# Turns of one operation for a background conversion, and the second head's preparation behind the second maximum, in a fused attention and expert kernel

## The chip, the cores and the metric

The kernel runs on one core of a Trainium2 chip. The metric is the time of one execution on the device in microseconds (us). Before the change the median of three runs is 1062.84 us (1062.28 to 1064.66). Engines are named as the profile names them: PE (TensorE, matrix products and transposes), DVE (VectorE), ACT (ScalarE), POOL (GpSimd), and SP, the queue that issues nearly all transfers.

## The reference

Three stages, each fed by the one before:

```python
q_pool = q.reshape(B, H, S // 2, 2, D).mean(axis=3)        # 4 x 8 heads, 576 pooled queries, D = 64
scores = np.matmul(q_pool, k.transpose(0, 1, 3, 2)) / sqrt(D)   # 576 x 1152
attn = softmax(scores);  x = attn @ v                      # 2304 rows of 512
# experts: 8, one per row by argmax of x @ w_gate, only rows with x @ w_skip > 0
x[rows] += gate * (relu(x[rows] @ w1[e]) @ w2[e])
# dense: out = ((x @ m1) * (x @ m2) @ w3) @ w_out          # weights arrive as 64-bit floats
```

## The kernel before

Attention fills the first half of the time. The 32 heads are taken in 16 pairs p of two heads, each pair in nine *tiles* l: eight of 128 queries of one head, and one (l = 4) with the last 64 queries of both. There are 144 tiles i = 9p + l, and the main loop takes two in a *step* (a = 0, 2, 4, ...). Products are made in fp32r from a high and a low part (a rounded copy, and what is left), so queries and keys are first split in two.

For one tile: PE multiplies queries by the keys (`emit_s`, L271) into three banks of PSUM, DVE finds the negated maximum of a row over all 1152 scores (`emit_x`, L282), ACT takes the exponential (`emit_e`, L294), PE transposes the result in nine pieces (`emit_t`, L305) into the three banks that the tile two further on will use for its scores, and ACT, DVE, ACT copy those three banks away (`emit_c`, L324: the second bank is DVE's). PE multiplies the copies by the values (`emit_pv`, L341).

Every engine works through its own instructions in the order in which the loop writes them. In step a this is: the exponentials of tiles a-2 and a-1; a turn of side work (the *first place*); the value products of earlier tiles; the 18 transposes of tiles a-2 and a-1 with their copies; a turn of side work again (the *second place*); the scores and maxima of tiles a and a+1. So DVE's order in a step is: first place, two copies, second place, two maxima.

Side work is of two kinds. The *routing* of a finished batch (`route_ops`) chooses experts, in pieces marked P (uses a PSUM bank), D (small DVE operations) and C. The *conversion* (`conv_ops`) turns the dense stage's 64-bit weights into 32-bit ones, in 40 chunks of 128 x 512 values: POOL squares the upper word (L96), and four DVE operations on data in SBUF make the result, L111 and L112 (mask and shift of the exponent), L116 (sign) and L119 (lower bits); SP stores it. A generator hands these out: an even chunk takes two turns (L111 with L112, L116 with L119), an odd chunk three (L111 with L112, L116, L119). Each place takes one turn, or a D piece of the routing in its stead.

At the start the first pair is prepared apart. `prep_q(h, DVE, 0, 256, ...)` and `prep_k(h, ...)` split the first 256 queries and the keys of head h on DVE (L203 to L207 and L197; ACT makes the keys' rounded copy, L196); POOL splits the other queries (same lines, POOL). For head 0 this stands ahead of the loop; for head 1, which tile 2 uses first, behind the scores and maximum of tile 0. `prep(1, 0)`, `prep(1, 1)` and `prep(1, 2)`, the split of the second pair's keys and queries, are POOL's (L224 to L238) and stand behind tiles 0, 1 and 2. Later pairs are split at tiles 6, 7 and 8 of the pair two before.

Of the kernel before, what the change touches and what calls it, by code (L numbers as in the profile page):

```python
# [17 lines left out]
NE, D, F = 8, 512, 1024  # L18
# [26 lines left out]
def body(ctx, tc, q, k, v, w9, w1, w2, m1, m2, w3t, wo, cst, mcst, ids, out, dbg=None):  # L45
# [3 lines left out]
    def f(t):  # L49
        return t.bitcast(F32)  # L50
# [37 lines left out]
    def conv_ops(erl):  # L88
        def ld(name, c):
            h = erl.tile([128, CW, 2], I32, tag="ch", name="ch", bufs=4)  # L90
            SP.dma_start(h, c_src(name, c))
            return h
        def sq(h):
            m = erl.tile([128, CW], F32, tag="cm", name="cm", bufs=3)
            hf = h.bitcast(F32)[:, :, 1]
            POOL.tensor_tensor(m, hf, hf, op=ALU.mult)  # L96
            return m

        nxt = [ld(*conv_q[i]) for i in range(3)]
        yield  # L100
        ms = [sq(nxt[0]), sq(nxt[1])]
        yield
        for n, (name, c) in enumerate(conv_q):
            h = nxt.pop(0)
            if n + 3 < len(conv_q):
                nxt.append(ld(*conv_q[n + 3]))
            a = erl.tile([128, CW], I32, tag="ca", name="ca", bufs=2)
            hf = h.bitcast(F32)[:, :, 1]
            m = ms.pop(0)
            u = m.bitcast(I32)  # L110
            DVE.scalar_tensor_tensor(m, m, TINY * TINY, hf, op0=ALU.is_ge, op1=ALU.mult)  # L111
            DVE.tensor_scalar(u, u, 0x07FFFFFF, 3, op0=ALU.bitwise_and, op1=ALU.logical_shift_left)  # L112
            yield
            if len(nxt) >= 2:
                ms.append(sq(nxt[1]))
            DVE.scalar_tensor_tensor(u, h[:, :, 1], -0x40000000, u, op0=ALU.bitwise_and, op1=ALU.bitwise_or)  # L116
            if n % 2:
                yield
            DVE.scalar_tensor_tensor(a, h[:, :, 0], 29, u, op0=ALU.logical_shift_right, op1=ALU.bitwise_or)  # L119
            c_dst(name, c, a.bitcast(F32))  # L120
            yield
# [13 lines left out]
    if True:  # L135
# [78 lines left out]
        def ld_kh(h):  # L214
            SP.dma_start(f(KH[0][64 * h:64 * h + 64]), f(KS[0][h][0:64]))

        def prep(p, j):
            if p >= NP:
                return
            i = p % 2  # L220
            if j == 0:
                for c in range(3):
                    cc = slice(384 * c, 384 * c + 384)
                    POOL.tensor_scalar(KH[i][:, cc], rawk[p][:, cc], 1.0, 0.0, op0=ALU.mult, op1=ALU.add)  # L224
                    POOL.tensor_tensor(KL[:, cc], rawk[p][:, cc], f(KH[i][:, cc]), op=ALU.subtract)  # L225
                del rawk[p]
            elif j == 1:
                qr = rawq.pop(p)
                s = pre[p] = erl.tile([128, SQ], F32, tag="qsum", name="qsum", bufs=1)
                POOL.tensor_tensor(s, qr[:, 0], qr[:, 1], op=ALU.add)  # L230
                POOL.tensor_scalar(s, s, 0.0625, 0.0, op0=ALU.mult, op1=ALU.add)
            elif j == 2:
                s = pre.pop(p)
                POOL.tensor_scalar(QN[0], s, 1.0, 0.0, op0=ALU.mult, op1=ALU.add)
                POOL.tensor_tensor(QN[1], s, f(QN[0]), op=ALU.subtract)
                for h in range(2):
                    r = slice(64 * h, 64 * h + 64)
                    POOL.tensor_scalar(BD[i][r, r], f(QN[1][r, 512:576]), 1.0, 0.0, op0=ALU.mult, op1=ALU.add)  # L238
            elif j == 3:
                for h in range(2):  # L240
                    r = slice(64 * h, 64 * h + 64)
                    for u, t in enumerate((KH[i], KL)):
                        SP.dma_start(f(KS[i][h][64 * u:64 * u + 64]), f(t[r]))
            else:
                for h in range(2):
                    r = slice(64 * h, 64 * h + 64)
                    for u in range(2):
                        d = slice(64 * u, 64 * u + 64)
                        if h == 0:
                            SP.dma_start(f(QS[i][h][0][d, 0:576]), f(QN[0][r]))  # L250
                        else:
                            SP.dma_start(f(QS[i][h][0][d, 0:512]), f(QN[0][r, 0:512]))
                            SP.dma_start(f(QS[i][h][0][d, 576:640]), f(QN[0][r, 512:576]))
                        SP.dma_start(f(QS[i][h][1][d]), f(QN[1][r]))
# [245 lines left out]
        conv = conv_ops(erl)  # L500
        rts = {}

        def side(kinds):
            k = rts.get("k")
            if k and k in kinds:
                rts["k"] = next(rts["g"], None)
            if kinds != "P" and k != "D":
                next(conv, None)

        def emit_meta(scratch):  # L510
# [240 lines left out]
        with tc.manual_schedule():  # L751
# [37 lines left out]
            for a in range(0, NSTEP + 8, 2):  # L789
                if a >= 44 and (a - 44) % 36 == 0 and (a - 44) // 36 < NB - 1:  # L790
                    rts["g"] = route_ops((a - 44) // 36)
                    rts["k"] = next(rts["g"])
                its = [i for i in (a - 2, a - 1) if 0 <= i < NSTEP]
                for i in its:
                    emit_e(i)
                route_step(a, 0)
                if a > 5:
                    side("DC")
                for pe in range(0, NP, 2):
                    for dp, hf, kt in PVU.get(a - 9 * pe, ()):  # L800
                        emit_pv(pe + dp, hf, kt)
                evac = {}
                for i in (a, a + 1):
                    if i < NSTEP or i - 2 in its:
                        st_s[i] = ps_s.tile([128, 3, 512], F32, tag="s", name="s")
                    evac[i] = []
                for i in its:
                    for g in range(3):
                        emit_t(i, g, i + 2, evac[i + 2])
                        emit_c(i, g, EV[g], evac[i + 2])  # L810
                if a > 5:
                    side("DC")
                route_step(a, 1)
                for i in (a, a + 1):
                    p, l = divmod(i, NT9)
                    ss = i < NSTEP
                    if i == NSTEP - NT9 + 1:
                        for _ in conv:
                            pass
                        ectx.close()  # L820
                        wfill = wprime_fill()
                    if i > NSTEP - NT9:
                        next(wfill, None)
                    if l == (4 if p == 0 else 1):
                        load(p + 2)
                    if l == 7 and p >= 1:
                        load_v(p + 1)
                    if ss:
                        for g in range(3):
                            emit_s(i, g, evac[i])  # L830
                        emit_x(i)
                        if i == 0:
                            prep_q(1, DVE, 0, 256, sq[1])
                            for c in range(3):
                                prep_k(1, 384 * c, 384 * c + 384)
                            ld_kh(1)
                            for h in range(2):
                                prep_q(h, POOL, 256, SQ, sr[h])
                            next(conv)
                            DVE.tensor_copy(base, cs[:, C_EOFF:C_EOFF + NC_])  # L840
                            DVE.tensor_copy(csr, cs[:, C_U:C_U + 256])
                        if i == 2:
                            PE.matmul(VB[1][:, 0:128], lhsT=ones, rhs=tri, start=True, stop=True)
                            DVE.tensor_copy(iota[:, 0:128], VB[1][:, 0:128])
                            DVE.tensor_scalar(iota[:, 128:NSL], iota[:, 0:NSL - 128], 128.0, None, op0=ALU.add)
                            DVE.tensor_scalar(idf, idt, 1.0, None, op0=ALU.add)
                    if ss and p == 0 and l < 3:
                        prep(1, l)
                    if i == 4:
                        next(conv)  # L850
                    if ss and l >= 6:
                        prep(p + 2, l - 6)
                    if ss and l in ((3, 4) if p == 0 else (4, 5)):
                        prep(p + 1, l if p == 0 else l - 1)
# [36 lines left out]
            n = 0  # L891
# [170 lines left out]
```

## Time and profile before

| what | value |
|---|---|
| median of three runs | 1062.84 us |
| the profiled execution | 1057.09 us |
| its span, first to last instruction | 1055.3 us |
| PE busy / DVE / ACT / POOL | 1003.0 / 600.0 / 460.7 / 386.7 us |
| mean granted TensorE clock | 0.988 of full |
| main loop (tiles) | until about 520 us of the span |

The profiled execution is one run of the program with the hardware profiler on, and lies 5.75 us under the median of the others. Busy time of PE counts matrix products that overlap; where PE waits, the row of its next instruction tells how long, and for whom.

### The profile page before, as it was taken

The numbers are of one execution on the slowest core, as the hardware profiler recorded it, in microseconds if no ns is written. First come the engines' busy times: TensorE is split into PE (matmuls) and PEld (weight loads), VectorE is DVE, ScalarE is ACT, GpSimd is POOL, SyncE is SP. The second block draws the span as 40 slices with busy tenths as digits, with TensorE's granted clock in tenths as the row PEclk, the third lists the DMA queues.
The fourth block names the chain that finished last, engine by engine and source line by source line (L and its number), as shares of the span: only waits on it lengthen the run. The fifth ranks groups of instructions, "written<-read, shape, count | busy, mean of one in ns | idle before, by whom it ended". The sixth has DMA issues, their size and how long they took to land. (4 is left out here: it accounts for less than half of the span.)

```text
span 1055.3 us, 16801 instructions
## 1 busy us (share of the span) xinstructions
PE 1003.0 (95%) x6101; PEld 834.5 (79%) x6101; DVE 600.0 (57%) x934; ACT 460.7 (44%) x902; POOL 386.7 (37%) x426
## 2 busy tenths in 40 slices
PE   4899999999999999999999999996999999999996
PEld 3677777777777777787778788874989898989895
DVE  5888988789889898866554424256523131313120
ACT  3566566655665566666522324254422121212120
POOL 4752444582536743460801625167111101010101
PEclk8999999999999999999989999998999999999999
DMA  9887878579964687743416723233101010110000
GB/s 263 225 237 210 241 214 216 164 191 246 253 197 149 193 253 210 191 117 116 159 40 224 279 62 135 97 138 129 31 20 41 25 37 31 31 37 24 30 1 32
DMA packets 68237, 144.82 MB, mean 137 GB/s; under 512 B 12960, under 2 KB 22560, under 8 KB 68130
## 3 DMA queue, kind: packets, MB, share of 16 engines
q1 hardware_dynamic: 63330, 129.28, 42.5%
q0 software_dynamic: 4800, 14.24, 4.1%
q8 instruction: 52, 0.85, 0.3%
q14 instruction: 55, 0.45, 0.1%
HBM read 86.21 MB, written 22.87 MB: 103 GB/s over the span
## 5 line engine op out<-in xcount | busy, mean ns | idle before, releaser
L294 ACT ACTIVATE p<-s,sm 128x1152 f32<-128x1152 f32 x144 | 175.9, 1221 | 183.3 <-DVE sm L282 183.3
L282 DVE TENSOR_REDUCE sm<-s 128x1 f32<-128x1152 f32 x144 | 189.1, 1349 | 20.2 <-PE s L271 17.6
L305 PEld LDWEIGHTS s<-cs,p 128*128 128x128 f32 x1296 | 140.3, 142 | 65.3 <-ACT p L294 57.7
L305 PE MATMUL s<-cs,p 128*128 128x128 f32 x1296 | 167.9, 279 | 21.7 <-ACT p L294 19.2
L271 PE MATMUL s<-k,q 128*128 128x384 f32 x864 | 178.6, 348 | 7.9 <-DVE k L197 7.7
L271 PEld LDWEIGHTS s<-k,q 128*128 128x128 f32 x864 | 149.9, 191 | 10.2 <-DVE k L197 8.2
L341 PE MATMUL vb<-pt,vr 128*64 128x256 f32 (+1 forms) x1152 | 155.1, 412 | 0.0
L972 DVE TENSOR_TENSOR ar<-b,ar 128x384 f32<-128x384 f32 x48 | 26.7, 557 | 192.2 <-PE b L968 192.2
L324 ACT COPY pt<-s 128x384 f32<-128x384 f32 x288 | 122.5, 491 | 11.3 <-PE s L305 9.2
L341 PEld LDWEIGHTS vb<-pt,vr 128*64 128x64 f32 x1152 | 76.5, 136 | 59.3 <-issue 15.4
L987 POOL DMA_INDIRECT out_dram<-ar,slots x18 | 18.0, 1000 | 272.4 <-ACT ar L986 267.7
L324 DVE COPY pt<-s 128x384 f32<-128x384 f32 x144 | 79.2, 555 | 64.5 <-PE s L305 63.8
L225 POOL TENSOR_TENSOR kl<-kr,kh 128x384 fp32r<-128x384 f32 x45 | 47.8, 1062 | 77.7 <-DMA k<-kl 75.0
L973 ACT CAST CVh<-ar 128x384 fp32r<-128x384 f32 x48 | 24.6, 513 | 108.5 <-DVE ar L972 108.5
L96 POOL TENSOR_TENSOR cm<-ch 128x512 f32<-128x512 f32 x40 | 44.2, 1110 | 65.2 <-DVE ca L119 42.0
L563 PE MATMUL b<-W1h,CVh 128*128 128x512 f32 x176 | 60.1, 402 | 0.9 <-ACT CVh L694 0.7
L563 PE MATMUL b<-W2h,CVh 128*128 128x512 f32 x176 | 60.7, 405 | 0.1
L563 PE MATMUL b<-WPh,CVh 128*128 128x512 f32 x144 | 57.3, 398 | 0.0
L563 PE MATMUL b<-WPh,CVl 128*128 128x512 f32 x144 | 56.9, 395 | 0.0
L563 PE MATMUL b<-WPl,CVh 128*128 128x512 f32 x144 | 56.8, 395 | 0.0
L986 ACT COPY ar<-b 128x512 f32<-128x512 f32 x18 | 10.5, 586 | 86.2 <-PE b L563 86.2
L224 POOL TENSOR_SCALAR kh<-kr 128x384 fp32r<-128x384 f32 x45 | 27.3, 606 | 46.3 <-PE s L271 45.3
(210 smaller groups left out, 1810.8 us busy)
## 6 DMA issues: line engine op xcount, KB each, us to landing
R<-in_w_dram SPq DMA_DIRECT2D x16, 1024.0 KB, 7.5
vr<-in_v_dram SPq DMA_DIRECT2D x16, 576.0 KB, 6.3
kr<-in_k_dram SPq DMA_DIRECT2D x15, 576.0 KB, 6.7
qr<-in_q_dram SPq DMA_DIRECT2D x15, 576.0 KB, 6.6
k<-kh SPq DMA_DIRECT2D x30, 288.0 KB, 5.6
k<-kl SPq DMA_DIRECT2D x30, 288.0 KB, 7.0
q<-qnl SPq DMA_DIRECT2D x60, 144.0 KB, 5.1
ch<-in_w3t_dram SPq DMA_DIRECT2D x16, 512.0 KB, 6.7
```

What stands on the lines that cost most here:

```text
L96: POOL.tensor_tensor(m, hf, hf, op=ALU.mult)
L224: POOL.tensor_scalar(KH[i][:, cc], rawk[p][:, cc], 1.0, 0.0, op0=ALU.mult, op1=ALU.add)
L225: POOL.tensor_tensor(KL[:, cc], rawk[p][:, cc], f(KH[i][:, cc]), op=ALU.subtract)
L271: m = PE.matmul(sp[:, c, 0:384], lhsT=lt, rhs=kk[:, 384 * c:384 * c + 384], start=(n == 0), stop=(n == len(seq) - 1))
L282: DVE.tensor_reduce(sm, sp[:, :, 0:384], axis=AX.XY, op=ALU.max, negate=True)
L294: ACT.activation(pt, sp[:, :, 0:384], AF.Exp, bias=sm, scale=1.0, accum_out=SM[b][:, hp, c:c + 1])
L305: m = PE.transpose(tp[:, u * 128:u * 128 + 128], src[:, kt * 128:kt * 128 + 128], ident)
L324: m = (DVE.tensor_copy(o, i_) if eng is DVE else ACT.copy(o, i_)).ins
L341: PE.matmul(acc[64 * h:64 * h + 64, 0:n], lhsT=vr[:, h, kt, :], rhs=pt[:, kt, h, :], start=(kt == 0), stop=(kt == KT - 1))
L563: PE.matmul(o, lhsT=lh[a], rhs=rh[b_], start=(first and n == 0), stop=(last and n == len(order) - 1))
L972: DVE.tensor_tensor(cv, pb[:, 0:GT], av, op=ALU.mult)
L973: ACT.copy(CV[0][:, c], cv)
```

## The change

Three edits. (1) The generator of the conversion gives control back after every one of its four DVE operations. (2) `side` takes a number of turns: two in the first place, one in the second; a D piece of the routing takes the place of one turn. The D piece itself is as before. (3) The preparation of head 1 of the first pair is written behind the scores and maximum of tile 1, not of tile 0, and the splits of the second pair on POOL behind tiles 1, 2 and 2, not 0, 1 and 2.

```diff
@@ conv_ops, for each chunk
             DVE.scalar_tensor_tensor(m, m, TINY * TINY, hf, op0=ALU.is_ge, op1=ALU.mult)
+            yield
             DVE.tensor_scalar(u, u, 0x07FFFFFF, 3, op0=ALU.bitwise_and, op1=ALU.logical_shift_left)
             yield
             if len(nxt) >= 2:
                 ms.append(sq(nxt[1]))
             DVE.scalar_tensor_tensor(u, h[:, :, 1], -0x40000000, u, op0=ALU.bitwise_and, op1=ALU.bitwise_or)
-            if n % 2:
-                yield
+            yield
             DVE.scalar_tensor_tensor(a, h[:, :, 0], 29, u, op0=ALU.logical_shift_right, op1=ALU.bitwise_or)
@@
-        def side(kinds):
+        def side(kinds, ops=0):
             k = rts.get("k")
             if k and k in kinds:
                 rts["k"] = next(rts["g"], None)
-            if kinds != "P" and k != "D":
+            if k == "D":
+                ops -= 1
+            for _ in range(ops):
                 next(conv, None)
@@ first place, then second place
-                    side("DC")
+                    side("DC", 2)
...
-                    side("DC")
+                    side("DC", 1)
@@
-                        if i == 0:
+                        if i == 1:
                             prep_q(1, DVE, 0, 256, sq[1])
                             for c in range(3):
                                 prep_k(1, 384 * c, 384 * c + 384)
...
                     if ss and p == 0 and l < 3:
-                        prep(1, l)
+                        prep(1, (l - 1) % 3) if l else None
+                        prep(1, 2) if l == 2 else None
```

DVE at the program's start, behind the split of head 0's keys (`k_119`). L282 is a maximum; L203 to L197 prepare head 1 (`ca` is scratch, `q_104`, `q_105`, `k_120` its queries and keys); L324 copies transposes of tiles 0 and 1 (`pt`). Before:

```order
L282 TENSOR_REDUCE sm<-s 128x1
L203 TENSOR_TENSOR ca<-qr 128x256
L204 TENSOR_SCALAR ca<-ca 128x256
L206 TENSOR_SCALAR q_104<-ca 128x256
L207 TENSOR_TENSOR q_105<-ca,q_104 128x256
L197 TENSOR_TENSOR k_120<-kl,k_120 64x384 x3
L840 COPY base<-cs 128x10
L841 CAST csr<-cs 128x256
L282 TENSOR_REDUCE sm<-s 128x1
L324 COPY pt_247<-s 128x3x128 x2
```

And now:

```order
L282 TENSOR_REDUCE sm<-s 128x1 x2
L203 TENSOR_TENSOR ca<-qr 128x256
L204 TENSOR_SCALAR ca<-ca 128x256
L206 TENSOR_SCALAR q_104<-ca 128x256
L207 TENSOR_TENSOR q_105<-ca,q_104 128x256
L197 TENSOR_TENSOR k_120<-kl,k_120 64x384 x3
L842 COPY base<-cs 128x10
L843 CAST csr<-cs 128x256
L324 COPY pt_244<-s 128x3x128 x2
```

The second maximum has moved ahead of the nine operations that prepare head 1 and two constants; the two copies stay behind them. PE's, ACT's and, up to the second pair's splits and the first three squares, POOL's orders at the start are what they were; so is SP's.

DVE in step a = 16 and a little behind it. L111, L112 (now L113), L116 (now L117) and L119 are the conversion's four operations, `pt` the copies of tiles 14 and 15. Before:

```order
L282 TENSOR_REDUCE sm<-s 128x1 x2
L111 SCALAR_TENSOR_TENSOR cm<-cm,ch 128x512
L112 TENSOR_SCALAR cm<-cm 128x512
L324 COPY pt_735<-s 128x3x128 x2
L116 SCALAR_TENSOR_TENSOR cm<-ch,cm 128x512
L119 SCALAR_TENSOR_TENSOR ca<-ch,cm 128x512
L282 TENSOR_REDUCE sm<-s 128x1 x2
```

And now:

```order
L282 TENSOR_REDUCE sm<-s 128x1 x2
L119 SCALAR_TENSOR_TENSOR ca<-ch,cm 128x512
L111 SCALAR_TENSOR_TENSOR cm<-cm,ch 128x512
L324 COPY pt_734<-s 128x3x128 x2
L113 TENSOR_SCALAR cm<-cm 128x512
L282 TENSOR_REDUCE sm<-s 128x1 x2
```

Between the copies and the maxima there stood two operations and now stands one; ahead of the copies there stand two in either. The last operation of the conversion stands one step earlier than it did (nine steps' maxima follow it in the place of eight).

## Rows read from the trace of the kernel before

**Rows 1.** The page's first line.

```profile
span 1055.3 us, 16801 instructions
```

**Rows 2.** Waits of PE, 36 to 495 us: us in total, times, longest.

```profile
PE s L305 <- ACT p L294: 9.7, 20, 1.6
...
PE s L271 <- DVE pt L324: 0.2, 1, 0.2
```

**Rows 3.** Timeline of DVE, two steps: start, us, line, operation, [idle before <-releaser].

```profile
64.33 0.68 DVE L119 SCALAR_TENSOR_TENSOR ca<-ch,cm 128x512 int32<-128x512 int32 x1
65.30 2.62 DVE L282 TENSOR_REDUCE sm<-s 128x1 f32<-128x1152 f32 x2 [0.28 <-PE s L271]
67.83 1.11 DVE L111 SCALAR_TENSOR_TENSOR cm<-cm,ch 128x512 f32<-128x512 f32 x1
...
70.73 1.28 DVE L116 SCALAR_TENSOR_TENSOR cm<-ch,cm 128x512 int32<-128x512 int32 x1
72.05 1.80 DVE L119 SCALAR_TENSOR_TENSOR ca<-ch,cm 128x512 int32<-128x512 int32 x1
73.77 2.61 DVE L282 TENSOR_REDUCE sm<-s 128x1 f32<-128x1152 f32 x2
```

**Rows 4.** Timeline of PE in the same steps.

```profile
70.30 2.33 PE L271 MATMUL s<-k,q 128*128 128x384 f32 x12
...
76.51 0.87 PE L305 MATMUL s<-cs,p 128*128 128x128 f32 x6 [1.57 <-ACT p L294]
```

**Rows 5.** Timeline of POOL beside the conversion of that step.

```profile
70.42 1.04 POOL L96 TENSOR_TENSOR cm<-ch 128x512 f32<-128x512 f32 x1
71.42 1.87 POOL L230 TENSOR_TENSOR qsum<-qr 128x576 f32<-128x576 f32 x1
```

**Rows 6.** Timeline of PE, 94 to 97 and 396 to 402 us.

```profile
96.27 0.98 PE L305 MATMUL s<-cs,p 128*128 128x128 f32 x7 [0.35 <-ACT p L294]
...
400.31 1.92 PE L305 MATMUL s<-cs,p 128*128 128x128 f32 x13 [0.23 <-ACT p L294]
```

**Rows 7.** Timeline of DVE, start of the program.

```profile
5.87 0.56 DVE L197 TENSOR_TENSOR k<-kr,k 64x384 fp32r<-64x384 f32 x1
...
11.77 0.42 DVE L203 TENSOR_TENSOR ca<-qr 128x256 f32<-128x256 f32 x1
...
13.34 2.42 DVE L197 TENSOR_TENSOR k<-kl,k 64x384 fp32r<-64x384 f32 x3
...
16.21 1.34 DVE L282 TENSOR_REDUCE sm<-s 128x1 f32<-128x1152 f32 x1
...
20.53 0.56 DVE L324 COPY pt<-s 128x384 f32<-128x384 f32 x1 [2.51 <-PE s L305]
23.16 1.36 DVE L282 TENSOR_REDUCE sm<-s 128x1 f32<-128x1152 f32 x1 [2.07 <-PE vb L843]
...
30.56 2.62 DVE L282 TENSOR_REDUCE sm<-s 128x1 f32<-128x1152 f32 x2 [1.41 <-PE s L271]
33.10 0.68 DVE L111 SCALAR_TENSOR_TENSOR cm<-cm,ch 128x512 f32<-128x512 f32 x1
...
35.97 1.54 DVE L116 SCALAR_TENSOR_TENSOR cm<-ch,cm 128x512 int32<-128x512 int32 x1
...
38.34 2.61 DVE L282 TENSOR_REDUCE sm<-s 128x1 f32<-128x1152 f32 x2
```

**Rows 8.** Timeline of PE, start of the program.

```profile
11.74 0.52 PE L271 MATMUL s<-k,q 128*128 128x384 f32 x1
...
20.78 2.27 PE L271 MATMUL s<-k,q 128*128 128x384 f32 x6
```

**Rows 9.** Timeline of POOL, start of the program.

```profile
13.74 0.88 POOL L203 TENSOR_TENSOR ch<-qr 128x320 f32<-128x320 f32 x1 [13.29 <-DMA qr<-in_q_dram]
...
31.10 3.58 POOL L96 TENSOR_TENSOR cm<-ch 128x512 f32<-128x512 f32 x3
```

**Rows 10.** Timeline of DVE, 320 to 325 us: a D piece in the first place.

```profile
321.36 1.42 DVE L405 TENSOR_TENSOR oh<-cs,cm 128x5 fp32r<-128x5 f32 x1
```

## The prediction

> **What bounds the kernel now.** I read the page's first line for the span, then who PE waited for in the main loop, then the timelines of DVE, PE and POOL side by side over two steps, then the same over the first 42 us. The profiled execution took 1057.09 us, 1055.3 of them span [rows 1] and 1.8 around it; the median of the three runs is 5.75 above it. I make the sum against the profiled execution and carry the difference to the median.
>
> In the main loop PE is nearly always at work. What it waits for there is the exponential: 20 waits, 9.7 us, between 36 and 495 us [rows 2]. The exponential waits for the maximum, and the maximum for DVE's turn. Step a = 16 shows how. The scores are made from 70.30 in twelve products of 0.19 [rows 4], so those of the first tile are there at 71.5; but DVE has two conversion operations ahead of the maxima, at 70.73 and 72.05, and gets to the maxima at 73.77 [rows 3]. That is 2.2 late, and PE pays 1.57 of it at 76.51 [rows 4]; the rest is hidden by the value products. In the step before, DVE had one operation in the second place (64.33, 0.68 us) and stood waiting 0.28 for PE when the scores came [rows 3].
>
> The two late operations are also long: 1.28 and 1.80 in place of 0.68 [rows 3]. The first ends at 72.01, 0.55 behind the end of POOL's square (70.42 + 1.04 = 71.46), the second at 73.85, 0.56 behind POOL's 1.87 us sum (ends 73.29) [rows 3, 5]. They stand until POOL's instruction is over and then do the rest of their work. So an operation in the second place costs 0.68 where POOL is idle and up to 1.8 where it is not, and the room there is 0.8 to 1.0: from DVE's second copy to the scores of the first tile, 70.73 to 71.5 here, 64.33 to 65.30 in the step before [rows 3].
>
> **The change, part by part.** *Second place: two operations become one.* By the turns before, three of five steps had two there, so 30 of the 50 that carried the conversion. I sorted the 20 waits by what stood in the second place one step earlier. Ten follow two operations, first 1.57 at 76.51, last 0.23 at 400.31 [rows 4, 6], 6.6 us together. Two follow one operation, 0.6 us. Seven, 2.1 us, lie ahead of transposes that only twelve value products precede (first 0.35 at 96.27 [rows 6]); those remain, as the chain from scores over maximum to exponential is longer than so little PE work whatever DVE does. The last, 0.4, belongs to the start below. Twenty steps with one operation thus left 0.6 us, 0.03 each. Some 50 steps of that kind leave 1.5, where there were 7.2: **-5.7**.
>
> *First place: always two, one beside a D piece.* In 20 of 50 steps this is one more than before, and in some 12 routing steps one where there was none. A first place may last about 2.3: it begins at 67.83, and the second bank of scores, which waits for DVE's first copy of 0.56, comes 0.4 behind 70.30 [rows 3, 4, 7]. Two operations of 0.68 fit, and so does one of 1.11 [rows 3] with a short one. It is tight beside a D piece whose own operation took 1.42 [rows 10]: three such steps, one per routing, with a further operation of 0.4 to 1.5. I take 0.3 us each, and 0.5 for the other steps together: **+1.4**; bounds 0 (all covered) and the rival below.
>
> Four operations a chunk and three a step instead of about 3.2 would make the conversion longer, but it no longer stops for the D pieces; its last operation comes one step sooner, and its stores with it, so nothing behind the loop waits for it. SP's stores move by a step at most; a store that SP waits for stands ahead of keys and queries that are needed several steps on.
>
> *The start.* The scores of tile 1 are done at 12.26 [rows 8], and its maximum, which ran at 16.21 behind head 1's preparation [rows 7], can run at 12.3 and be over at 13.65. The preparation, 11.77 to 16.21 before, 4.44 us, starts at 13.65 instead. POOL starts at 13.74 [rows 9], so all of it lies beside POOL now. Three of its operations did so already and took 2.42, 0.81 each, where the same one alone takes 0.56 [rows 7]; 0.25 more for each of the other four is 1.0. The preparation ends at 19.1, the two copies at 20.2 (the second ended at 21.09 before [rows 7]). The second bank's scores of tile 2 can start at 19.7. Six such products took 2.27 at 20.78, half of the full rate [rows 8, 4]; four more take 0.8 to 1.5, so tile 2's maximum starts at about 20.9 and not at 23.16 [rows 7]: 2.3 earlier.
>
> Then comes a wait that was not there. From that maximum to the end of tile 5's there are 10.0 us (23.16 to 30.56 + 2.62), so DVE gets to its first conversion operation at 30.9. It needs a square from POOL, whose three from 31.10 take 1.19 each [rows 9]: 32.3. POOL's own chain begins with a transfer and is not moved. DVE stands 1.4 us, with the copies of tiles 4 and 5, and so PE, behind it. Of the 2.3 us 0.8 is left (32.3 against 33.10 [rows 7]). The second place follows 2.87 later as before, at 35.2, has one operation of 1.54 in the place of two, and the maxima start at 36.7, not 38.34: **-1.6**. Bounds: -0.6 if POOL is held up 1 us by DVE, -3.4 if tile 2 comes 2.6 earlier and DVE need not wait. Moving the second pair's splits one tile on changes nothing in POOL's order, and costs nothing.
>
> The sum: -5.7 + 1.4 - 1.6 = -5.9. The profiled execution would take 1051.2, and the median be 1062.84 - 5.9 = **1056.9 us**.
>
> **The rivals.** *POOL turns the start round.* If each of the seven preparation operations stood through a whole POOL instruction, up to 0.88 [rows 9], four would cost 0.63 more than I took and three 0.63 more than they did, 4.4 in all. Tile 2's maximum would come at 25.3, 2.1 late, and POOL, held up in turn by some 3 us of DVE work, would square that much later. With 0.8 saved in the next second place the start costs 1.5 or so, and the total is -2.8: 1060.0. For it: rows 3 and 5, where two operations did wait like that. Against: the three that lay beside POOL in this very stretch lost 0.25 each [rows 7]. The Trainium skill, page "SBUF — State Buffer", section "Who interferes with whom", has this as a rule: a VectorE instruction with two inputs in SBUF and a GpSimd instruction that reads SBUF exclude each other for the whole instruction. By that rule alone this rival is the outcome; the stretched pair of step 16 agrees with it to 0.01 us, the 2.42 us for three does not show its full price.
>
> *Nothing comes of it.* The waits move: DVE does the same work in a stage where PE takes 6.5 to 8 us a step anyway, one operation meets POOL's longest instruction as often as two did, and the start is eaten by the wait for the square. Then -1 to +1: 1062.8. Against it speak the twenty steps with one operation, which leave 0.6 us.
>
> *Slower: the first place runs over.* Where both of its operations meet POOL they take 1.28 + 1.80 = 3.1 [rows 3], 0.8 more than the room; PE stands between transposes and scores, and the maxima are late as well, 0.9 us a step. POOL splits a pair for some 11 us out of every four and a half steps, so about 20 steps are exposed. From 7 of them on the gain is gone, at 10 it is +9 - 5.9 = +3.1: 1065.9. Against it: two operations stood in the first place in 30 steps before, beside the same POOL work, and PE waited for DVE's copy once, for 0.2 us [rows 2].
>
> **How the numbers follow.** Forecast 0.56, its own range 1054.5 to 1060 (loop -3 to -6.5, start -0.6 to -3.4). Start turned round 0.20, nothing 0.13, first place over 0.11. About 0.2%, 2.1 us, is what a measurement of this kernel can tell from no change: faster means below 1060.7, slower above 1065.0. Faster: 0.55 of the forecast and 0.15 of the turned start, 0.70. Same: the rest of these two, 0.05, and most of the third, 0.12: 0.18 with a little of the last. Slower: 0.12. The range for 8 in 10 reaches from 1053.0, where both bounds are met, to 1063.2, which takes in the first two rivals.
>
> **What would show it.** After the change PE's waits for the exponential between the same steps should be near 4 us (2.1 that remain, 1.5 and a few at routing steps) and not 9.7. DVE's idle time ahead of the maxima, ended by PE, should grow. The second maximum should start at about 12.3 and tile 2's near 21; L111 of the first chunk should show an idle time of about 1.4 ended by POOL's square. I am wrong if PE waits for L324 in many steps (first place over), if the preparation of head 1 takes over 7 us (start turned round), or if the maxima start no sooner behind the scores than they did.

## The result, and the profile after

The changed kernel takes 1051.34 us (median of 4 runs, 1050.81 to 1053.51) against 1062.56 us of the kernel before: ratio 0.9902, interval 0.9879 to 0.9926. In a second comparison, with more runs of before, it is 0.9910 (0.9891 to 0.9929). The forecast had the direction; the time lies 5.6 us below it and 1.7 us below its range. One run of an experiment below (e_three) took 1998.1 us, nearly twice its eleven others; why is open, and it is left out of the figures.

First the page's first line of the changed kernel, then its waits of PE between 36 and 495 us (us in total, times, longest), which answer to [rows 1, 2].

```profile
span 1049.9 us, 16795 instructions
```

```profile
PE s L305 <- ACT p L294: 3.2, 9, 0.7
PE s L271 <- DVE pt L324: 0.5, 2, 0.2
```

Twenty waits for the exponential became nine, 9.7 us became 3.2. The waits for DVE's copies, where the forecast put its cost, went from 0.2 to 0.5. The weight loads of the same transposes (PEld in the rows, PE's loading of its weights; 42 to 500 us, grouped by line: busy, mean ns, then idle time and what ended it), of the kernel before and of the changed one:

```profile
L305 PEld LDWEIGHTS s<-cs,p 128*128 128x128 f32 x1179 | 126.9, 141 | 51.2 <-ACT p L294 43.6 <-issue 5.6 <-ACT lgp L368 1.0
```

```profile
L305 PEld LDWEIGHTS s<-cs,p 128*128 128x128 f32 x1193 | 128.6, 141 | 43.2 <-ACT p L294 33.6 <-issue 7.5 <-ACT lgp L368 1.5
```

What the exponential holds up fell by 10.0 us here, more than the 6.5 us by which PE's waits fell. The rows for the waits of PE show the stop ahead of the first transpose; the loads also count one between the two tiles' transposes, of which more below, and idle time that the value products still cover, so the 10.0 is no sum of what PE lost.

The step of [rows 3, 4] after the change, on DVE (start, us, line, operation, idle before):

```profile
66.56 1.50 DVE L111 SCALAR_TENSOR_TENSOR cm<-cm,ch 128x512 f32<-128x512 f32 x1
67.98 1.01 DVE L324 COPY pt<-s 128x384 f32<-128x384 f32 x2
68.91 0.90 DVE L113 TENSOR_SCALAR cm<-cm 128x512 int32<-128x512 int32 x1
69.82 2.62 DVE L282 TENSOR_REDUCE sm<-s 128x1 f32<-128x1152 f32 x2
72.36 0.78 DVE L117 SCALAR_TENSOR_TENSOR cm<-ch,cm 128x512 int32<-128x512 int32 x1
73.18 1.79 DVE L119 SCALAR_TENSOR_TENSOR ca<-ch,cm 128x512 int32<-128x512 int32 x1
```

and on PE:

```profile
68.42 2.33 PE L271 MATMUL s<-k,q 128*128 128x384 f32 x12
70.69 2.37 PE L341 MATMUL vb<-pt,vr 128*64 128x320 f32 x16
72.99 2.18 PE L305 MATMUL s<-cs,p 128*128 128x128 f32 x18
74.93 1.35 PE L271 MATMUL s<-k,q 128*128 128x384 f32 x5
```

One operation of 0.90 stands in the second place, the maxima start at 69.82, 1.4 behind the scores' start (3.5 before [rows 3, 4]), and where PE stood 1.57 the transposes follow the value products without a stop. The first place now holds the stretched operation (1.79 at 73.18), and the next scores at 74.93 don't wait for it.

The start, DVE, answering to [rows 7]:

```profile
12.42 1.36 DVE L282 TENSOR_REDUCE sm<-s 128x1 f32<-128x1152 f32 x1 [0.56 <-PE s L271]
...
14.26 0.84 DVE L204 TENSOR_SCALAR ca<-ca 128x256 f32<-128x256 f32 x1
...
16.34 3.17 DVE L197 TENSOR_TENSOR k<-kl,k 64x384 fp32r<-64x384 f32 x3
...
21.58 1.36 DVE L282 TENSOR_REDUCE sm<-s 128x1 f32<-128x1152 f32 x1 [0.66 <-PE vb L845]
...
30.36 2.62 DVE L282 TENSOR_REDUCE sm<-s 128x1 f32<-128x1152 f32 x2 [1.83 <-PE s L271]
32.90 1.14 DVE L111 SCALAR_TENSOR_TENSOR cm<-cm,ch 128x512 f32<-128x512 f32 x1
...
36.07 0.70 DVE L117 SCALAR_TENSOR_TENSOR cm<-ch,cm 128x512 int32<-128x512 int32 x1
36.81 2.62 DVE L282 TENSOR_REDUCE sm<-s 128x1 f32<-128x1152 f32 x2
```

The second maximum comes at 12.42 (forecast 12.3), head 1's preparation lasts from 13.80 to 19.5, or to 19.9 with the two constants that the forecast's 19.1 includes, tile 2's maximum starts at 21.58 (20.9). Then the lead shrinks: tiles 4 and 5 have their maxima at 30.36, 0.2 ahead of before. Between lie PE's transposes, and a low granted clock, 0.54 of full speed from 24 to 29 us, so near the lower of its two levels (1.2 GHz). The timeline of PE, then PE's stretch (from and to, us, busy, granted clock, DMA share, GB/s):

```profile
24.34 4.24 PE L305 MATMUL s<-cs,p 128*128 128x128 f32 x18 [1.12 <-ACT p L294]
```

```profile
24.00:29.00 5.00, 4.66 (x21) 0.54 1.02 350
```

Eighteen transposes take 4.24 here and 2.18 in the loop. In the kernel before, the same transposes and the same stretch:

```profile
25.91 1.21 PE L305 MATMUL s<-cs,p 128*128 128x128 f32 x9 [1.65 <-ACT p L294]
27.67 1.20 PE L305 MATMUL s<-cs,p 128*128 128x128 f32 x9 [0.55 <-ACT p L294]
```

```profile
24.00:29.00 5.00, 2.80 (x22) 1.00 1.04 350
```

Its low granted clock (0.50) lay earlier, from 18 to 22 us, and these transposes ran at the full one. So the changed kernel begins them 1.57 sooner and ends them only 0.3 sooner. Its other two traces record 0.66 and 0.55 from 24 to 29 us; of the other four of before, three record 1.00 and one 0.93.

### The profile page after: what moved, and what is told of

It is laid out like the page before. It is cut to its first block, busy times and chain, and to the rows that moved or that the text cites. A ratio compares the mean times of both kernels' runs of the same rounds, so it can differ in the third digit from the quotient of the medians.

```text
span 1049.9 us, 16795 instructions
## 1 busy us (share of the span) xinstructions
PE 1005.7 (96%) x6101; PEld 837.3 (80%) x6101; DVE 600.7 (57%) x934; ACT 462.8 (44%) x902; POOL 388.5 (37%) x426
## 5 line engine op out<-in xcount | busy, mean ns | idle before, releaser
L294 ACT ACTIVATE p<-s,sm 128x1152 f32<-128x1152 f32 x144 | 176.0, 1222 | 168.9 <-DVE sm L282 168.9
L282 DVE TENSOR_REDUCE sm<-s 128x1 f32<-128x1152 f32 x144 | 189.5, 1352 | 30.7 <-PE s L271 29.7
L305 PEld LDWEIGHTS s<-cs,p 128*128 128x128 f32 x1296 | 143.1, 143 | 51.5 <-ACT p L294 41.4
L271 PEld LDWEIGHTS s<-k,q 128*128 128x128 f32 x864 | 149.8, 191 | 13.5 <-DVE k L197 8.3
L324 ACT COPY pt<-s 128x384 f32<-128x384 f32 x288 | 124.2, 491 | 15.0 <-PE s L305 11.6
L324 DVE COPY pt<-s 128x384 f32<-128x384 f32 x144 | 78.8, 554 | 44.7 <-PE s L305 44.0
```

Of the source, the lines that this page charges most:

```text
L271: m = PE.matmul(sp[:, c, 0:384], lhsT=lt, rhs=kk[:, 384 * c:384 * c + 384], start=(n == 0), stop=(n == len(seq) - 1))
L282: DVE.tensor_reduce(sm, sp[:, :, 0:384], axis=AX.XY, op=ALU.max, negate=True)
L294: ACT.activation(pt, sp[:, :, 0:384], AF.Exp, bias=sm, scale=1.0, accum_out=SM[b][:, hp, c:c + 1])
L305: m = PE.transpose(tp[:, u * 128:u * 128 + 128], src[:, kt * 128:kt * 128 + 128], ident)
L324: m = (DVE.tensor_copy(o, i_) if eng is DVE else ACT.copy(o, i_)).ins
```

## The experiments

Where the traces are compared below, the *loop* is the time from the start of tile 6's exponential to that of tile 142's (line L294 on ACT), what is ahead of it is the *start*, and from there to the span's end is *the rest*.

### One edit at a time

*The turns alone* (e_turns): the changed kernel with the start put back.

```diff
-                        if i == 1:
+                        if i == 0:
                             prep_q(1, DVE, 0, 256, sq[1])
...
-                        prep(1, (l - 1) % 3) if l else None
-                        prep(1, 2) if l == 2 else None
+                        prep(1, l)
```

> The turns alone, start as before. Theory 'second place' (the gain is one operation instead of two between the copies and the second place's maxima, plus the second exponential's wait among the transposes): all of the loop's gain of about 8 us from step 8 on stays, so 1052 to 1053, and the loop's last transposes 8 +- 1 us ahead of before's. Theory 'start' (the earlier preparation carries the gain, which stays ahead because the loop has slack): 1058 or more, the loop less than 3 us ahead. The forecast on record, by its own terms, gave the turns alone -4.3: 1058.5 against before's 1062.8.

*The start alone* (e_start): the same two places changed on the kernel before.

> The start alone, turns as before. Theory 'second place': the gain is what the first trace of after shows at step 8, 0.6 us, so 1062 (ratio 0.999 to 1.000). Theory 'start': at least half of the 11 us, so 1057 or less. The forecast's start term gave -1.6: 1061.0.

Measured in one comparison: e_turns 1053.44 (ratio 0.9919, 0.9900 to 0.9938), e_start 1059.57 (0.9989, 0.9971 to 1.0008), the changed kernel again (a_again) 1051.50, before again (b_again) 1059.51. The turns carry the gain, with a loop of 469.9 us in the trace of e_turns and 475.8 in that of e_start; the start alone can't be told from nothing. The waits of PE, 36 to 495 us, of e_turns and of e_start:

```profile
PE s L305 <- ACT p L294: 3.5, 10, 0.6
```

```profile
PE s L305 <- ACT p L294: 7.0, 18, 0.9
```

### Three operations a step, placed otherwise

*Turned round* (e_swap): one operation in the first place, two in the second.

```diff
-                    side("DC", 2)
+                    side("DC", 1)
...
-                    side("DC", 1)
+                    side("DC", 2)
```

> The changed kernel with the turns the other way round: one operation in the first place, two in the second; still three a step. Theory 'second place': now some 50 steps have two operations between the copies and the maxima where before had 30, so TensorE's waits for the exponential in the loop are at least those of before (8.6 and 11.5 us in its two traces), perhaps up to 5/3 of them, 19; the median is 1060 to 1067 and the runs spread over 5 us or more as before's do (1056 to 1065). Theory 'evenness' (the gain comes from three in every step in place of two or four): the median stays at 1051 to 1054, the spread below 4 us.

Measured: 1066.43, ratio 1.0060 (1.0038 to 1.0082). Slower than before.

```profile
PE s L305 <- ACT p L294: 13.5, 29, 1.5
```

*All in the first place* (e_three): `side("DC", 3)` and `side("DC", 0)`.

> The changed kernel with all three operations in the first place and none in the second. Theory 'second place' in full: no step has an operation ahead of the maxima, so waits for the exponential fall to the seven steps with twelve value products and the start (under 4 us); but three operations of 0.68 are 2.04, beside POOL's work up to 3.5, against a room of 2.3, so TensorE waits for the vector engine's copies in 10 to 20 steps, 0.3 to 1 us each: 1053 to 1062. If the room in the first place is larger than the forecast took it, the copies cost nothing and the time is 1050 to 1052. Theory 'evenness': 1051.5, as the changed kernel.

Measured: 1058.58, ratio 0.9988 (0.9974 to 1.0001). Waits of PE, and one such step on DVE and PE:

```profile
PE s L271 <- DVE pt L324: 6.1, 11, 1.7
PE s L305 <- ACT p L294: 2.5, 8, 0.4
```

```profile
68.23 0.68 DVE L119 SCALAR_TENSOR_TENSOR ca<-ch,cm 128x512 int32<-128x512 int32 x1
68.83 1.50 DVE L111 SCALAR_TENSOR_TENSOR cm<-cm,ch 128x512 f32<-128x512 f32 x1
70.36 1.52 DVE L113 TENSOR_SCALAR cm<-cm 128x512 int32<-128x512 int32 x1
71.81 1.01 DVE L324 COPY pt<-s 128x384 f32<-128x384 f32 x2
```

```profile
70.69 0.60 PE L271 MATMUL s<-k,q 128*128 128x384 f32 x2
72.40 2.00 PE L271 MATMUL s<-k,q 128*128 128x384 f32 x10 [1.11 <-DVE pt L324]
```

Three operations of 3.6 us together push the copies to 71.81, and PE stands 1.11 for the second bank. So the same three operations cost 15 us more than the change in one order and 7 more in the other. "Evenness" falls; the two rooms, ahead of the copies and ahead of the maxima, are what counts, and two and one is what fits them.

### What makes two operations late

POOL's splits of pairs 2 to 15 made on 32 columns, on the kernel before (b_pool) and on the changed one (a_pool). Most of the splitting is left out; only the loops are compared.

```diff
+                w = 384 if p == 1 else 32
...
-                    cc = slice(384 * c, 384 * c + 384)
+                    cc = slice(384 * c, 384 * c + w)
...
-                POOL.tensor_tensor(s, qr[:, 0], qr[:, 1], op=ALU.add)
+                POOL.tensor_tensor(s[:, :w], qr[:, 0, :w], qr[:, 1, :w], op=ALU.add)
```

(and so on for the other three operations of the queries)

> The kernel before, with POOL's splits of pairs 2 to 15 made on 32 columns of each piece instead of 384 or 576 (it leaves out most of the splitting; keys and queries of those pairs are then partly old ones, so the routing and the expert stage differ, and only the loop is compared). Theory 'two operations are late because they stand by POOL's long instructions': two operations now take their 0.7 each, 1.4 against a room of 0.8 to 1.0, late by 0.5, which the value products hide: waits for the exponential in the loop fall from 8.6 to 11.5 us to 3 to 4, and the loop's last transposes come at 504 to 506 us in place of 510 to 512. Rival, the count alone: two operations are too many whatever POOL does, and the waits stay above 7 us.

> The changed kernel with POOL's splits of pairs 2 to 15 narrowed as in the kernel before (most of the splitting is left out; only the loop is compared). With the narrowed splits the kernel before lost its loop 7.1 us (b_again to b_pool), waits 3.2 us in 36 to 495. If the turns matter only because two operations stand by POOL's long instructions, the turns bring 1 us or less here: waits 2.5 to 3.5 us, the loop's last transposes within 1.5 us of the other narrowed kernel's. If the count matters by itself, the turns still bring half of their 6 us or more: 3 us earlier.

The two operations in the second place of step 16, in before again and in b_pool:

```profile
70.63 1.48 DVE L116 SCALAR_TENSOR_TENSOR cm<-ch,cm 128x512 int32<-128x512 int32 x1
72.14 1.42 DVE L119 SCALAR_TENSOR_TENSOR ca<-ch,cm 128x512 int32<-128x512 int32 x1
```

```profile
69.05 0.68 DVE L116 SCALAR_TENSOR_TENSOR cm<-ch,cm 128x512 int32<-128x512 int32 x1
69.77 0.69 DVE L119 SCALAR_TENSOR_TENSOR ca<-ch,cm 128x512 int32<-128x512 int32 x1
```

Waits of PE in b_pool, 36 to 495 us:

```profile
PE s L308 <- ACT p L297: 3.2, 10, 0.5
```

The loop of b_pool takes 468.1, that of a_pool 466.3; with full splits the means of the traces below are 477.5 and 469.6. So the turns are worth 7.9 us beside POOL's long instructions and 1.8 without them (one trace each, and traces of before differ by up to 4.6). The operations' number alone costs little; that they stand until POOL is done is what makes them late. The Trainium skill, page "SBUF — State Buffer", section "Who interferes with whom", says of operations that contend, as one of DVE with two inputs in SBUF does with one of POOL that reads SBUF, that whoever of the two engines comes first holds the shared pair for its whole instruction and the other is blocked; 1.48 beside POOL against 0.68 with POOL idle for the same operation agrees.

### What the conversion still costs

a_noconv leaves out the four operations and POOL's squares.

```diff
-            DVE.scalar_tensor_tensor(m, m, TINY * TINY, hf, op0=ALU.is_ge, op1=ALU.mult)
             yield
...
-            c_dst(name, c, a.bitcast(F32))
+            c_dst(name, c, a)
```

> The changed kernel without the conversion's four operations and without POOL's squares (its loads and stores stay, the stored values are a constant): what the conversion still costs after the change. Theory 'second place': the seven waits ahead of transposes behind twelve value products stay (about 2 us), the other few vanish: 1047.5 to 1050 overall, one or two us of it in the start. Rival: the conversion still holds TensorE up by stretching the copies and maxima it stands beside; then 1045 or less. Rival: the seven waits are the conversion's too; then they vanish as well.

Measured: 1044.13 (4 runs), loop 464.9.

```profile
PE s L296 <- ACT p L285: 2.8, 8, 0.7
```

The waits behind twelve value products are no matter of the conversion: all seven are there without it, 2.1 of the 2.8 us. The time is the one that the first rival gave (1045 or less), but its reason does not hold: the maxima and copies beside the conversion are not stretched. DVE's maxima in the changed kernel and in a_noconv, 42 to 500 us (busy, mean ns, then idle time before them):

```profile
L282 DVE TENSOR_REDUCE sm<-s 128x1 f32<-128x1152 f32 x132 | 173.5, 1352 | 24.6 <-PE s L271 24.3
```

```profile
L273 DVE TENSOR_REDUCE sm<-s 128x1 f32<-128x1152 f32 x134 | 176.2, 1352 | 53.7 <-PE s L262 53.1 <-issue 0.7
```

1352 ns in both; DVE's copies take 554 and 558. 4.7 us of loop remain to be had. Over steps 8 to 142, 0.7 of them lie ahead of the first transpose and 2.2 between it and the first score; the other 1.8 were not found.

### Does the profiled execution stand for the others?

The profiled pair had moved by 5.4 us only, the medians by 9 to 11. Unchanged kernels again:

> The kernel before, unchanged, for a second trace of it. If the traces so far stand for the kernels, its profiled run again shows 20 waits of TensorE for the exponential between 36 and 495 us (9.7 us together). The four timed runs of before lie between 1060.3 and 1064.7, its profiled one at 1057.1: if that 5 us lies in the expert stage (after 555 us) and comes and goes with the run, the loop of this trace (position of the same transposes at the end of the attention loop, 512.0 us before) should be within 1 us of the old trace, while the end differs by some us. If it lies in the loop, the loop's end moves instead.

> The changed kernel, unchanged, for a second trace: 1051.3 +- 1. The loop's last transposes at 503.3 +- 1 us as in the first trace, ten first waits for the exponential (5.0 us) between 30 and 490 us. If the profiled pair (5.4 us apart) and the medians (11.2 apart) differ by chance in the expert stage, the stage after 555 us of this trace and of the second trace of before tell how far it varies from run to run of one kernel.

> The kernel before, a third profiled execution. If its profiled runs are a chance draw from its timed runs (64 of them so far lie between 1056 and 1065 with a median of 1061), the three further ones lie about that median, at least one of them above 1060, and their loops (from tile 6's exponential to tile 142's, 477.0 and 475.0 us in the two traces so far) vary with them, by waits for the exponential between 8 and 13 us. If profiling itself makes this kernel faster, all three lie at 1057 to 1058.5 with loops of 475 to 477.

> The kernel before, a fourth profiled execution: as for the third. By chance: about 1061, with more than half of the difference from the faster traces in the loop's waits. If profiling makes it faster: 1057 to 1058.5.

> The kernel before, a fifth profiled execution: as for the third. By chance: about 1061. If profiling makes it faster: 1057 to 1058.5.

> The changed kernel, a third profiled execution: 1050.5 to 1053, its loop 469 to 470 us as in the two traces so far (469.9, 469.2), whichever of the two holds for the kernel before.

| trace | time | start | loop | rest |
|---|---|---|---|---|
| before | 1057.09 | 39.7 | 477.0 | 538.6 |
| b_again | 1057.63 | 40.1 | 475.0 | 540.8 |
| b_r3 | 1059.48 | 39.6 | 476.7 | 541.4 |
| b_r2 | 1064.70 | 39.7 | 479.5 | 543.7 |
| b_r4 | 1065.11 | 41.6 | 479.3 | 542.4 |
| after | 1051.69 | 38.2 | 469.9 | 541.9 |
| a_again | 1052.77 | 39.8 | 469.2 | 542.1 |
| a_r2 | 1049.22 | 38.9 | 469.8 | 538.8 |

By chance, then: the five profiled runs of before spread from 1057 to 1065 as its timed ones do. Waits of PE for the exponential come to 6.8 to 11.7 us in the five and to 3.1 to 3.3 in the three of the changed kernel. They are, in the slowest of before and in the third trace of the changed kernel, 36 to 495 us:

```profile
PE s L305 <- ACT p L294: 11.7, 20, 1.8
```

```profile
PE s L305 <- ACT p L294: 3.1, 9, 0.6
```

The loop of before varies by 4.6 us from run to run, that of the changed kernel by 0.7. Which operation meets which instruction of POOL differs from run to run (the two in the second place of step 16 took 1.28 and 1.80 in one trace of before, 1.48 and 1.42 in another). That this makes the loop vary, and no longer does with one operation there, fits the waits but was not tested by itself. The rest varies by 5 us in before and 3 in the changed kernel and is the same on average (541.4 and 540.9). The means differ by 1.2 in the start (40.1, 39.0), 7.9 in the loop (477.5, 469.6), 0.5 in the rest: 9.6 us. All 84 runs of before have a median of 1060.9, the 11 of the changed kernel 1051.5.

### Versions that might beat both

*The value products spread anew* (v_pv), so that the step with twelve follows nine score products.

```diff
-                   12: [(0, 1, k) for k in range(4)], 14: [(0, 1, k) for k in range(4, 8)],
+                   12: [(0, 1, k) for k in range(4)], 14: [(0, 1, k) for k in range(4, 7)],
...
-                   24: [(1, 1, k) for k in range(6, 9)]}
+                   24: [(1, 1, k) for k in range(5, 9)]}
```

> The changed kernel with the value products of a double pair spread anew: the step with twelve of them is moved from the place behind a short step of scores to the place behind a step whose second tile has nine score products. If the seven waits (0.23 to 0.36 each, 2.1 us, and as much again 0.28 each where the second tile's exponential is waited for among the transposes) are a matter of too little work between the scores and the transposes, they go: 1047.5 to 1050, the loop 3 to 4 us shorter. If the waits only move to the new step: 1051.5 again.

Measured: 1051.29. The waits moved. Step 14 on PE:

```profile
58.19 1.52 PE L341 MATMUL vb<-pt,vr 128*64 128x256 f32 x12
59.63 1.20 PE L305 MATMUL s<-cs,p 128*128 128x128 f32 x9
61.12 1.20 PE L305 MATMUL s<-cs,p 128*128 128x128 f32 x9 [0.28 <-ACT p L294]
```

The first tile's transposes come in time, the second tile's wait 0.28 for the second exponential. Over steps 8 to 142 the first kind of wait fell from 3.6 (mean of the changed kernel's traces) to 1.5, and the time from the first transpose to the first score, summed over the steps, rose from 152.0 to 154.6.

*The start's small operations later* (v_start), and *with products in PE's idle time* (v_warm), both on v_pv.

```diff
+                        if i == 3:
+                            for _ in range(7):
+                                PE.matmul(VB[0][:, 0:384], lhsT=QS[0][0][0][:, 0:128], rhs=KS[0][0][:, 0:384],
+                                          start=True, stop=True)
                             DVE.tensor_copy(base, cs[:, C_EOFF:C_EOFF + NC_])
                             DVE.tensor_copy(csr, cs[:, C_U:C_U + 256])
-                        if i == 2:
                             PE.matmul(VB[1][:, 0:128], lhsT=ones, rhs=tri, start=True, stop=True)
```

(the `for` and the product below it in v_warm alone)

> As v_pv, and with the vector engine's small operations of the start (the two casts of constants ahead of the copies of step 2, 0.4 us, and the three of the slot numbers between the maxima of tiles 2 and 3, 1.3 us) placed behind the maximum of tile 3, where the vector engine waited 2.5 us for TensorE's second transposes. If the maxima set the start's pace, tile 3's maximum starts 1.2 to 1.7 us earlier and the loop with it: 1 to 1.5 us below v_pv. If TensorE's granted clock in the start or POOL's squares set it, no more than 0.3 us below v_pv.

> As v_start, with seven products into an unused bank behind the scores of tile 3, while TensorE waits for the exponential of tile 2 (they leave no result). In the traces so far 9 or 18 of the transposes behind that wait ran at half rate (18 in 4.24 us instead of 2.2). If the granted clock follows TensorE's idle time, the transposes run at full rate and the start is 0.5 to 1.5 us shorter than v_start's. If not, or if something else is late by then, the same as v_start; up to 0.5 us more if the products themselves delay the transposes.

Measured: 1051.88 and 1053.04. In v_start the move was ill made: PE's product for the slot numbers went along, and stood ahead of the transposes until DVE's cast behind tile 3's maximum. In v_warm the transposes ran at full rate, and DVE then stood by POOL's square, as the forecast had it for the change itself. They did so in v_pv too, without the products (1.20 for each nine, granted clock 0.96 from 24 to 29 us), so that one trace of each doesn't show what the products did. PE in v_start, PE and DVE in v_warm:

```profile
26.19 0.33 PE L845 MATMUL vb<-csr 128*128 128x128 f32 x1 [2.62 <-DVE csr L844]
```

```profile
24.68 2.15 PE L305 MATMUL s<-cs,p 128*128 128x128 f32 x18
```

```profile
33.69 1.51 DVE L111 SCALAR_TENSOR_TENSOR cm<-cm,ch 128x512 f32<-128x512 f32 x1 [2.55 <-POOL cm L96]
```

*Both mended* (v_s2, on the changed kernel: the product stays behind tile 2, and the conversion is taken up at step 8, not 6), and with the products (v_w2).

```diff
-                if a > 5:
+                if a > 7:
...
                             PE.matmul(VB[1][:, 0:128], lhsT=ones, rhs=tri, start=True, stop=True)
+                        if i == 3:
                             DVE.tensor_copy(iota[:, 0:128], VB[1][:, 0:128])
```

> The changed kernel with two edits in the start: the vector engine's three operations on the slot numbers (1.4 us) behind the maximum of tile 3 instead of ahead of it, TensorE's product for them left where it was; and the conversion taken up at step 8 instead of step 6, so that the vector engine doesn't stand before POOL's first square (2.55 us in v_warm). If the maxima set the start's pace: tile 3's maximum 1.2 to 1.4 us earlier, the transposes of step 8 1 to 2 us ahead of the changed kernel's (40.5 to 42.1): 1049 to 1050.5. If the transposes' half rate takes the gain, or the second pair's keys are late by then: 1051.5 as the changed kernel.

> As v_s2, with seven products into an unused bank behind the scores of tile 3. If TensorE's granted clock follows its idle time there, the 18 transposes of step 4 take 2.2 us and not 3.4 to 4.2, and the start is 1 to 2 us shorter than v_s2's: 1048 to 1049.5. If something else is late by then: the same as v_s2.

Measured: 1050.31 (1047.35 to 1052.53) and 1050.79 (1048.83 to 1052.48), not to be told from the changed kernel's 1051.5. Transposes of step 4, v_s2 and v_w2:

```profile
25.27 4.32 PE L305 MATMUL s<-cs,p 128*128 128x128 f32 x18 [0.73 <-ACT p L294]
```

```profile
25.53 1.15 PE L305 MATMUL s<-cs,p 128*128 128x128 f32 x9
26.90 1.20 PE L305 MATMUL s<-cs,p 128*128 128x128 f32 x9 [0.23 <-ACT p L294]
```

The start of v_w2 is 37.6, 1.4 shorter than the changed kernel's mean, that of v_s2 39.4, none. That the start's gain was lost at the half rate of these transposes and, without that, at the square, fits these traces; but there is one of each, 1.4 us is less than the runs' own spread, and the loop goes the other way: 469.6 in v_w2 and 466.2 in v_s2, 3 us below any trace of the changed kernel, for a reason that stays open.

## Why the forecast fell short

Two terms of the sum failed. The first place was given a cost of 1.4 that no row asked for, and the stop of PE for the second tile's exponential, among the transposes, was put at nothing; it gave back 2.0. What the sum was carried to, the median of three runs, was 1.9 too high besides.

*Second place, -5.7: right.* Summed over steps 8 to 142, PE's waits ahead of the first transpose are 9.7 on average in the five traces of before and 3.6 in the three after: -6.1. e_swap and e_three move the same waits to 13.5 and 2.5 (by the view of waits), and the pair of narrowed splits shows why two are late.

*What the forecast left out: -2.0.* "One operation instead of two" also brings the second tile's maximum forward, and with it the second exponential, for which PE stops between the ninth transpose and the tenth (a step's transposes take up to 0.28 more where it does). From first transpose to first score the steps take 154.0 us in sum before and 152.0 after. The forecast counted only the waits for the exponential that the view of waits lists ahead of a group of transposes; the weight loads' row shows both. In e_three and a_noconv the same sum falls further, to 150.4 and 149.8; in e_swap it rises to 155.8.

*First place, +1.4: did not come.* Waits for L324 are 0.2 to 1.3 us before and 0.3 to 0.5 after. The reason given, a room of about 2.3, was sound: three operations overrun it (6.1 us), two fit even when one takes 1.79. The 0.3 for each D piece and the 0.5 for the rest were a margin that no row asked for. The rival "first place runs over" is the case of three operations, not of two.

*The start, -1.6: the number met by luck, the gain of the earlier preparation not shown.* Half of the term was the lead that the preparation should bring (0.8), half the single operation in the next second place (0.8). In the first pair of traces the lead at the first conversion operation is 0.2 (32.90 against 33.10 [rows 7]) and the second place gives 1.3, so that the maxima start at 36.81, near the 36.7 forecast. What failed is the 10.0 us that the forecast carried over from tile 2's maximum to the end of tile 5's: they became 11.4 (21.58 to 32.98), as the transposes between fell into the stretch of low granted clock. On average the starts of the traces differ by 1.2, with a spread of 1.6 to 2.0 from run to run; but e_turns, without the earlier preparation, has a start of 38.7, and e_start, with it alone, 39.5. The wait for POOL's square did not show, since the maxima came later than the square; v_warm shows such a wait. The rival "POOL turns the start round" fell: the seven operations of the preparation grew from 4.0 to 5.7 us (with the two constants from 4.4 to 6.1), where the forecast had 5.4 with the constants and the rival 9.9. The four that were alone before took the 1.0 more that was forecast, the three subtractions another 0.75. The agreement to 0.01 us that the forecast names there is one of two remainders with each other (0.55 and 0.56 behind POOL's end).

*Carried to the median: 1.9 us off.* The profiled execution was a low one and the three timed ones high ones of the same spread, 1056 to 1065; the forecast took their difference of 5.75 as fixed. Against the median of all 84 runs, 1060.9, the same sum gives 1055.0, still above each of the 11 runs of the changed kernel (1049.2 to 1054.1).

Together, of the 5.6 us by which the forecast lay too high: loop 3.6 (-7.9 in place of -4.3), start -0.4 (-1.2 in place of -1.6), rest 0.5, the three runs' median 1.9.

## What to carry to other kernels

Work that fills an engine's gaps goes into the gap that is long enough in the worst case, beside the other engine's longest instruction, and not evenly; the short gap ahead of the operation that the critical engine waits for gets one piece or none. Count every place at which the critical engine stops for a late result, also in the middle of a group, before pricing it. Where a kernel's runs spread over more than the gain in question, sum against several traces, since the one at hand may be a good or a bad draw.

## What the runs showed of the hardware

- A conversion operation with two inputs (128x512) took 0.67 to 0.71 us in all 446 cases in which POOL was idle (36 to 515 us, eight traces of the two kernels). Beside POOL it took 0.67 to 1.98, with a median of 0.82 to 0.85: about half of the meetings cost DVE nothing to speak of, and those that do cost up to 1.3. The operation on a single input (L113, L112 before) is stretched too: 0.41 to 0.43 with POOL idle, up to 1.88 beside it.
- The loop of one unchanged program took 475.0 to 479.5 us, and 469.2 to 469.9 with one operation moved out of the second place.
- At the start the granted clock was low (0.50) from 18 to 22 us in the trace of before and from 22 to 28 in that of the changed kernel. Ahead of that PE had stood 3.46 us (to 18.95) in the first, 1.70 (to 20.51) and 1.12 (to 24.34) in the second. The transposes of step 4 took 2.4 us in before, at 1.00, and 4.24 in the changed kernel, at 0.54.
- The record of the clock and the rate don't always agree: the changed kernel's transposes at 14.32 took 4.10 at a recorded 1.00 (14 to 18 us), those of step 4 in v_s2 4.32 at 1.00 (25 to 30 us). So the clock explains the 4.24 above and is not shown for these two.
